# The two arms of a branch in the middle of a fused attention and expert kernel change places

## The chip, the cores and the metric

The kernel runs on one core of a Trainium2 chip. A core has five engines with their own instruction streams: TensorE (PE; its weight loads are shown as PEld), VectorE (DVE), ScalarE (ACT), GpSimd (POOL) and SyncE (SP, which issues most DMAs). A row with a q behind the engine's name is an instruction of that engine's sequencer: a branch, a wait, a DMA issue. The metric is device time in microseconds for one execution.

## The reference

A random-feature attention feeds a layer of eight experts of which each row takes one. There are 4 batches of 576 rows, 8 heads of 64, 2304 rows of 512 in all. Cut to what matters:

```python
proj = np.einsum('bhsd,md->bhsm', x, omega)          # for q and k, scaled
h = proj - sum(x * x) / 2
phi = np.exp(h - h.max(-1)) / np.sqrt(m)
kv = np.einsum('bhsm,bhsd->bhmd', k_p, v)
attn = einsum('bhsm,bhmd->bhsd', q_p, kv) / (einsum('bhsm,bhm->bhs', q_p, k_p.sum(2)) + 1e-06)

logits = x @ w_gate                                   # x: attn as 2304 rows of 512
expert_idx = np.argmax(logits, axis=1)
# the first `capacity` rows of each expert are kept, the others give zero rows
h = np.maximum(x_kept @ w1[e], 0.0)                   # 512 -> 1024
out[i] = gate_w[i] * (h @ w2[e])                      # 1024 -> 512
```

## The kernel before

The attention comes first: keys and values in 18 steps, then queries in 18 steps of 128 rows, with matrix products in float32 on 128 x 128 tiles. Its result goes to a DRAM buffer, and the logits of the experts fall out of the same products.

The expert part works on *items*. An item is a block of 576 rows (SLOTS) that goes through one expert: `mm1` makes the hidden layer in 16 steps, each of 4 x 3 matmuls, since every operand is split into a high and a low part (names ending in hi and lo); `second` makes the five output tiles with `upper` (L898, L899), `lower` (L904) and `rest` (L908), and `finish` scales a tile on ACT (L936) and hands it to `put` (L972), which sends it out by a DMA, four from SP's queue and the fourth tile's from ACT's. Item 0 is the first batch with the expert of row 0. While it runs, the routing is computed, which decides how the other rows are served. Two numbers come out of it, both read from `resd` into registers of every engine: `nd` (L1106), the number of further whole batches in which one expert serves rows, and `nl` (L1107), the number of rows that are left over for such items.

`item` is a generator. The code draws four pieces of item 0 from it (BRANCH_AT is 4), and then branches at L1108 on `nl`. The arm for left-over rows, called the list arm here, writes lists of rows by expert and works through them in up to 11 nested steps, `if ng > 0`, `if ng > 1` and so on, each with its own copy of the code of an item. The other arm draws the rest of item 0 (its last output tile) and then up to three further items, in nested tests `if nd > 0`, `if nd > 1`, `if nd > 2`. Each of these bodies is unrolled. A conditional is built as blocks in every engine's program: a compare-and-branch, the true block right behind it, an unconditional branch at its end, and the false block behind that. A nested test without an else has a small false block too, which brings the semaphores to where the true block would have left them.

With the inputs given `nl` is 0, so the list arm is not taken, and two further items run: `nd` is 2, and the third nested test is false.

The order of instructions is that in which the code is written (a manual schedule). At the end each engine comes to the closing code of L1199: SP waits for all that is outstanding, each engine drains, and POOL collects the others' signals and lets all of them go.

Of the kernel before, what the change touches and what calls it, by code (L numbers as in the profile page):

```python
# [19 lines left out]
B, H, S, D, M = 4, 8, 576, 64, 128  # L20
# [43 lines left out]
def attention_moe(ctx, tc, kT, qT, va, om, wg, w1, w2, cap, ident, tri, desc, lst, tab0, out):  # L64
# [276 lines left out]
    def zero_out(k):  # L341
        if k == 0:
            nc.sync.dma_start(out[SLOTS : SLOTS + REST, :], zero_sb[0:REST, :])
            return
        t = NSUB + 7 * (k - 1)
        z = min(t + 7, NT)
        nc.sync.dma_start(
            out[t * 128 : z * 128, :].rearrange("(a p) d -> p a d", p=128),
            zero_sb.unsqueeze(1).to_broadcast([128, z - t, DM]),
        )  # L350
# [20 lines left out]
    def load_w(i, c, ev, chunks_of="(p k)"):  # L371
        if i == 1:
            src = w1[ds(ev, 1), :, c * 256 : (c + 1) * 256].rearrange(f"o {chunks_of} f -> p (o k) f", p=128)
        else:
            src = w2[ds(ev, 1), c * 256 : (c + 1) * 256, :].rearrange("o (k p) f -> p (o k) f", p=128)
        nc.sync.dma_start(w_raw[i][c], src)

    def split_w_hi(i, c, eng=None):
        split_hi(w_hi[i][c], w_raw[i][c], eng)

    def split_w_lo(i, c, eng=nc.vector, k=None):
        sl = slice(None) if k is None else slice(k, k + 1)
        split_lo(w_lo[i][c][:, sl, :], w_raw[i][c][:, sl, :], w_hi[i][c][:, sl, :], eng)

    def load_idx(start):
        nc.sync.dma_start(big["idx"], tab_d[ds(start, SUB * NSUB), :].rearrange("(i p) c -> p i c", p=SUB))
# [11 lines left out]
    def load_x(rows, b0=0):  # L398
        src = x_d[rows, :].rearrange("(b r) (q c) -> q r b c", r=32, q=4)
        for q in range(4):  # L400
            nc.sync.dma_start(big["xz"][32 * q : 32 * q + 32, b0:, :], src[q])
# [294 lines left out]
    def mm1(f, n, hhi, hlo, hr, nm):  # L696
        xhi, xlo = big["xhi"], big["xlo"]
        whi_, wlo_ = w_hi[1][f // 2], w_lo[1][f // 2]
        fs = slice((f % 2) * 128, (f % 2) * 128 + 128)
        a, z = HALVES[n]  # L700
        sl = slice(a, z)
        pt = bank(turn[0] % 3, f"h{nm}{f}{n}")[:, 0 : z - a]
        turn[0] += 1
        for k in range(4):
            nc.tensor.matmul(pt, whi_[:, k, fs], xhi[:, k, sl], start=(k == 0), stop=False)  # L705
            nc.tensor.matmul(pt, wlo_[:, k, fs], xhi[:, k, sl], start=False, stop=False)  # L706
            nc.tensor.matmul(pt, whi_[:, k, fs], xlo[:, k, sl], start=False, stop=(k == 3))  # L707

        def take():
            w = min(z, 4 * SUB) - a  # L710
            sl = slice(a, a + w)
            parts = [(hhi[:, f, sl], hlo[:, f, sl], pt[:, 0:w])]
            if n == 1:
                parts.append((hr[:, f, 0:REST], hr[:, f, REST:], pt[:, w:]))
            for hi, lo, src in parts:
                nc.scalar.activation(hi, src, AF.Relu)  # L716
            for hi, lo, src in parts:
                nc.vector.scalar_tensor_tensor(lo, src, 0.0, hi.bitcast(F32), op0=ALU.max, op1=ALU.subtract)  # L718

        return take  # L720
# [228 lines left out]
    def listing(n):  # L949
        stop[0] = None  # L950
        for _ in range(n):
            if stop[0] is None:
                stop[0] = next(il, 0)
                if stop[0] == 0:
                    return
# [3 lines left out]
    def item(j):  # L959
        nonlocal row, row_a  # L960
        nm = f"i{j}"
        last = j == B - 1
        hhi, hlo, hr = h0
        if j > 0:
            row_a = nc.scalar.value_load(resd[0:1, 1, j - 1 : j], min_val=0, max_val=N - S)
        out_j = [out[0:SLOTS, :]] * 2 if j == 0 else [out[ds(r, SLOTS), :] for r in (row, row_a)]
        sc = sc_b[:, 0, :] if j == 0 else sc_j[:, j - 1, :]

        def put(i, n, y, out_j=out_j):

            k = int(i == NSUB - 2)
            (nc.sync, nc.scalar)[k].dma_start(out_j[k][i * SUB : i * SUB + n, :], y[0:n, :])  # L972

        def prefetch():
            nonlocal row
            if last:
                return
            ev = nc.sync.value_load(resd[0:1, 0, j : j + 1], min_val=0, max_val=E - 1)
            row = nc.sync.value_load(resd[0:1, 1, j : j + 1], min_val=0, max_val=N - S)
            load_x(ds(row, SLOTS))  # L980
            for c in range(4):
                load_w(1, c, ev)
            evs.append(ev)
            yield

        pre = prefetch()
        for k, (f, half) in enumerate(STEPS[j > 0]):
            mm1(f, half, hhi, hlo, hr, nm)()
            if j == 0:

                listing(5 if k > 4 else 1)
            if 0 < j < B - 1 and k == 0:
                for c in range(4):
                    load_w(2, c, evs[-1])
            if j > 0 and k == 4:
                next(pre, 0)
            if j == 0 and k < 3:
                zero_out(k)
            if half == 0:
                continue  # L1000
            for i, c in HI_AT[j > 0].get(f, ()):
                split_w_hi(i, c)
            for i, c in LO_AT[j > 0].get(f, ()):
                split_w_lo(i, c)
        if j == 0:
            for _ in il:
                pass
            next(pre, 0)
        def ready(c):
            split_w_hi(1, c)  # L1010
            split_w_lo(1, c)

        if 0 < j and not last:
            turn_x(0, NBA)()
            ready(0)
            turn_x(NBA, NB)()
            ready(1)
        if j == B - 2:
            for c in range(4):
                load_w(2, c, evs[-1])  # L1020
        for n, (i, pt) in enumerate(second(hhi, hlo, hr, nm)):
            first_x = turn_x(0, NBA) if j == 0 and n == 1 else None
            finish(i, pt, nm, sc[:, i : i + 1], put)
            if first_x is not None:
                first_x()
            yield

            if j == 0 and n == 2:
                ready(0)
                last_x = turn_x(NBA, NB)  # L1030
                ready(1)
                last_x()
# [69 lines left out]
    first = item(0)  # L1102
    for k in range(BRANCH_AT):
        next(first)
        if k == 1:
            nd = nc.values_load(resd[0:1, 2, 0:1], min_val=0, max_val=B - 1)  # L1106
            nl = nc.values_load(resd[0:1, 2, 1:2], min_val=0, max_val=N)  # L1107
    with ExitStack() as ifs:  # L1108
        cond = ifs.enter_context(tc.If(nl > 0))
        for t in range(BRANCH_AT - 1, NSUB - 1):  # L1110
            nc.sync.dma_start(out[t * SUB : (t + 1) * SUB, :], zero_sb)
        make_lists()
        ng = nc.values_load(res[0:1, 0, 15:16], min_val=0, max_val=NJ)
        for j in range(J):
            nm = f"l{j}"
            ifs.enter_context(tc.If(ng > j))
            ev = nc.sync.value_load(res[0:1, 0, j : j + 1], min_val=0, max_val=E - 1)
            sv = nc.sync.value_load(res[0:1, 1, j : j + 1], min_val=0, max_val=(E - 1) * REG + N)
            load_idx(sv)
            for c in range(4):  # L1120
                load_w(1, c, ev, "(k p)")
            for c in range(4):
                load_w(2, c, ev)
            gather()
            hhi, hlo, hr = h0
            for c in range(4):
                split_w_hi(1, c)
                split_w_lo(1, c)
            for i in range(NSUB):
                for _ in transpose_x(i, nm, SM if i % 2 else None):  # L1130
                    pass
            for f in range(8):
                for half in range(2):
                    mm1(f, half, hhi, hlo, hr, nm)()
                if f % 2:
                    split_w_hi(2, f // 2)
                    split_w_lo(2, f // 2)
            for i, pt in second(hhi, hlo, hr, nm):
                finish(i, pt, nm, idx[:, i, 1:2].bitcast(F32), put_rows)
    with cond.Else():  # L1140
        for _ in first:
            pass
        with ExitStack() as ifs:
            for j in range(1, B):
                ifs.enter_context(tc.If(nd > j - 1))
                for _ in item(j):
                    pass


# [53 lines left out]
```

## Time and profile before

| | us |
|---|---|
| median of 3 runs | 261.96 (260.59 to 262.24) |
| profiled execution | 260.95 |
| its span, first to last instruction | 259.2 |
| PE busy in the span | 253.7 |
| start of the branch at L1108, POOL first, SP last | 130.5 to 151.5 |
| PE's last eight matmuls | 253.38 to 255.36 |

The span is that of the profiled execution; the time that is compared also holds what lies around it, here 1.75 us. Sequencer rows (PEldq, ACTq, ...) are not counted as busy. Where an engine stands still after a branch, no row says so: it is read from the start of its next row.

### The profile page before, as it was taken

What the parts mean: (1) busy time and instruction counts of PE and PEld (TensorE: products, weight loads), DVE (VectorE), ACT (ScalarE), POOL (GpSimd) and SP (SyncE); (2) the same over time, 40 slices, a digit from 0 to 9 for tenths busy, and PEclk for the clock granted to TensorE, in tenths of its full rate; (3) what the DMA queues carried; (4) which work ended last, traced back from release to release, by engine and by line L of the source; (5) the groups of instructions that cost most, each with busy time, mean ns of one, the idle gap of its engine ahead of it and who ended that gap; (6) DMA issues with size and microseconds to landing.
All of it is one profiled execution on the core that took longest, in us unless ns stands there. A gap on an engine that the chain in (4) does not pass through costs nothing. (4 is left out here: it accounts for less than half of the span.)

```text
span 259.2 us, 7581 instructions
## 1 busy us (share of the span) xinstructions
PE 253.7 (98%) x3058; PEld 232.7 (90%) x3058; DVE 167.2 (65%) x351; ACT 148.8 (57%) x374; POOL 42.6 (16%) x61
## 2 busy tenths in 40 slices
PE   7999999999999999999999999999999999999994
PEld 6999999999999999999988789999888999998882
DVE  3999888779999998655763745566850064667500
ACT  3788888899999995326402536552361155524611
POOL 1002000255369896200000000000000000000000
PEclk9999999999999999999999999999999999999999
DMA  7999870034976769990059619992012897950121
GB/s 204 390 382 349 285 254 3 5 122 149 311 234 207 275 169 289 373 390 21 1 134 276 206 49 311 213 286 66 3 40 66 293 245 206 326 164 0 49 93 48
DMA packets 35171, 48.54 MB, mean 187 GB/s; under 512 B 2290, under 2 KB 23410, under 8 KB 35122
## 3 DMA queue, kind: packets, MB, share of 16 engines
q1 hardware_dynamic: 34002, 46.39, 57.0%
q10 hardware_dynamic: 1120, 1.52, 1.9%
q8 instruction: 28, 0.46, 0.7%
q14 instruction: 21, 0.17, 0.2%
HBM read 35.97 MB, written 11.93 MB: 185 GB/s over the span
## 5 line engine op out<-in xcount | busy, mean ns | idle before, releaser
L705 PE MATMUL hi<-xhi,w1hi 128*128 128x256 f32 (+1 forms) x192 | 56.7, 295 | 0.0
L706 PE MATMUL hi<-xhi,w1lo 128*128 128x256 f32 (+1 forms) x192 | 56.4, 294 | 0.0
L707 PE MATMUL hi<-xlo,w1hi 128*128 128x256 f32 (+1 forms) x192 | 56.3, 293 | 0.0
L718 DVE SCALAR_TENSOR_TENSOR hlo<-hi,hhi 128x256 fp32r<-128x256 f32 x48 | 20.2, 420 | 44.4 <-ACT hhi L716 22.4
L716 ACT ACTIVATE hhi<-hi 128x256 fp32r<-128x256 f32 x48 | 18.3, 384 | 36.1 <-PE hi L707 36.1
L898 PE MATMUL yi<-w2hi,hhi 128*128 128x512 f32 x96 | 37.5, 390 | 0.3 <-issue 0.3
L899 PE MATMUL yi<-w2hi,hlo 128*128 128x512 f32 x96 | 37.4, 389 | 0.0
L705 PEld LDWEIGHTS hi<-xhi,w1hi 128*128 128x128 f32 x192 | 36.0, 188 | 0.3
L706 PEld LDWEIGHTS hi<-xhi,w1lo 128*128 128x128 f32 x192 | 36.0, 188 | 0.1
L707 PEld LDWEIGHTS hi<-xlo,w1hi 128*128 128x128 f32 x192 | 36.0, 187 | 0.0
L192 DVE TENSOR_REDUCE mx<-pjk 128x4 f32<-128x512 f32 (+1 forms) x38 | 23.4, 656 | 4.2 <-PE pjk L175 4.0
L837 POOL TENSOR_TENSOR d<-d,mx 128x512 f32<-128x512 f32 x18 | 18.7, 1039 | 42.2 <-DVE mx L192 39.8
L175 PE MATMUL pjk<-om_s,kraw 64*128 64x128 f32 x288 | 23.9, 300 | 0.2
L818 ACT ACTIVATE ex<-pjk,mx 128x128 f32<-128x128 f32 x72 | 20.6, 368 | 6.0 <-DVE mx L192 5.7
L904 PE MATMUL yi<-w2lo,hhi 128*128 128x512 f32 x96 | 23.7, 389 | 0.0
L654 PE MATMUL qacc<-kv_sb,qpT 128*64 128x73 f32 x576 | 22.5, 230 | 0.1
L898 PEld LDWEIGHTS yi<-w2hi,hhi 128*128 128x128 f32 x96 | 18.0, 188 | 4.3 <-issue 0.7
L175 PEld LDWEIGHTS pjk<-om_s,kraw 64*128 64x128 f32 x288 | 20.4, 203 | 1.5 <-DMA kraw<-kT 0.6
L175 PE MATMUL pjq<-om_s,qraw 64*128 64x128 f32 x288 | 21.6, 284 | 0.0
L904 PEld LDWEIGHTS yi<-w2lo,hhi 128*128 128x128 f32 x96 | 18.0, 188 | 3.7
L899 PEld LDWEIGHTS yi<-w2hi,hlo 128*128 128x128 f32 x96 | 18.0, 188 | 3.6
L852 ACT ACTIVATE d<-pjq,mx 128x128 f32<-128x128 f32 x72 | 21.0, 404 | 0.3 <-DVE mx L192 0.3
(148 smaller groups left out, 416.4 us busy)
## 6 DMA issues: line engine op xcount, KB each, us to landing
w1raw<-w SPq DMA_DIRECT2D x16, 512.0 KB, 6.8
w2raw<-w SPq DMA_DIRECT2D x16, 512.0 KB, 5.8
qraw<-qT SPq DMA_DIRECT2D x6, 768.0 KB, 6.3
x_d<-xr SPq DMA_DIRECT2D x18, 256.0 KB, 4.3
v<-va SPq DMA_DIRECT2D x7, 650.0 KB, 6.5
xg<-x_d SPq DMA_DIRECT2D x12, 288.0 KB, 7.6
kraw<-kT SPq DMA_DIRECT2D x5, 576.0 KB, 7.0
out<-ysi SPq DMA_DIRECT2D x9, 256.0 KB, 2.1
```

What stands on the lines that cost most here:

```text
L175: nc.tensor.matmul(banks[i][:, k * M : (k + 1) * M], parts[k][rows, :], om_s[rows, :], start=True, stop=True)
L192: nc.vector.tensor_reduce(mx[:, a : a + src.shape[1]], src, op=ALU.max, axis=AX.X, negate=True)
L654: nc.tensor.matmul(acc[i][r : r + 64, p * ROW : (p + 1) * ROW], qpT[:, r // 64, (4 * i + p) * 64 : (4 * i + p) * 64 + 64], kv_sb[(t * 128 ...
L705: nc.tensor.matmul(pt, whi_[:, k, fs], xhi[:, k, sl], start=(k == 0), stop=False)
L706: nc.tensor.matmul(pt, wlo_[:, k, fs], xhi[:, k, sl], start=False, stop=False)
L707: nc.tensor.matmul(pt, whi_[:, k, fs], xlo[:, k, sl], start=False, stop=(k == 3))
L718: nc.vector.scalar_tensor_tensor(lo, src, 0.0, hi.bitcast(F32), op0=ALU.max, op1=ALU.subtract)
L818: nc.scalar.activation(ex[:, o + k, :], q[0][:, k * M : (k + 1) * M], AF.Exp, bias=mx[:, o + k : o + k + 1], scale=1.0)
L852: nc.scalar.activation(d[:, 4 + k, :], pj[1][:, k * M : (k + 1) * M], AF.Identity, bias=mx[:, 4 + k : 5 + k], scale=1.0)
L898: nc.tensor.matmul(pt, hhi[:, f, sl], w2_at(w_hi, f), start=(f == 0), stop=False)
L899: nc.tensor.matmul(pt, hlo[:, f, sl], w2_at(w_hi, f), start=False, stop=False)
L904: nc.tensor.matmul(pt, hhi[:, f, sl], w2_at(w_lo, f), start=False, stop=(f == 7))
```

## The change

The condition is turned round (`nl > 0` becomes `nl < 1`), and the blocks with it: the rest of the items is now the true block, which stands right behind the compare-and-branch, and the list arm is the else block behind it. The bodies are the same, and so are the semaphores and the number of instructions on each engine. In the new file the outer test is still at L1108, the nested tests over items are at L1111 (before at L1143), those of the list arm at L1116 (before at L1108).

```diff
-    with ExitStack() as ifs:
-        cond = ifs.enter_context(tc.If(nl > 0))
+    with tc.If(nl < 1) as cond:
+        for _ in first:
+            pass
+        with ExitStack() as ifs:
+            for j in range(1, B):
+                ifs.enter_context(tc.If(nd > j - 1))
+                for _ in item(j):
+                    pass
+    with cond.Else(), ExitStack() as ifs:
         for t in range(BRANCH_AT - 1, NSUB - 1):
             nc.sync.dma_start(out[t * SUB : (t + 1) * SUB, :], zero_sb)
         make_lists()
...
-    with cond.Else():
-        for _ in first:
-            pass
-        with ExitStack() as ifs:
-            for j in range(1, B):
-                ifs.enter_context(tc.If(nd > j - 1))
-                for _ in item(j):
-                    pass
```

On PE, around the outer test, the program of before has the list arm right behind the branch (xtrl is a tile of that arm; yi is an output tile of an item, yl one of the list arm), and the rest of item 0 some 3150 rows further on:

```order
L904 MATMUL yi_2800<-w2lo_2317,hhi 128x512 x2
L1108 COMPARE_AND_BRANCH
L1113 TENSOR_LOAD ilres
L1108 COMPARE_AND_BRANCH
L420 MATMUL xtrl_2977<-id_sb,xg 128x128 x4
...
L904 MATMUL yl_8230<-w2lo_2317,hhi 128x512 x2
L1108 UNCONDITIONAL_BRANCH x12
L898 MATMUL yi_8260<-w2hi_2310,hhi 128x512
L899 MATMUL yi_8260<-w2hi_2310,hlo 128x512
```

In the changed program the rest of item 0 follows the branch:

```order
L904 MATMUL yi_2800<-w2lo_2317,hhi 128x512 x2
L1108 COMPARE_AND_BRANCH
L898 MATMUL yi_2829<-w2hi_2310,hhi 128x512
L899 MATMUL yi_2829<-w2hi_2310,hlo 128x512
L898 MATMUL yi_2829<-w2hi_2310,hhi 128x512
```

The list arm has moved from between these rows to behind the items. On ACT, at the end of the last nested item (item 3, the one that is not run here), the program of before ends with the final branches of the items' arm, and the closing code follows them directly:

```order
L936 ACTIVATE ysi_9577<-yi_9552,sc_j 128x512
L936 ACTIVATE ysi_9605<-yi_9580,sc_j 128x256
L972 ISA
L972 DMA out<-ysi_9605 128x512
L1143 UNCONDITIONAL_BRANCH x4
```

In the changed program the list arm follows those branches (its first load, its first nested test, its first casts), some 485 rows of it, and the closing code stands behind them:

```order
L936 ACTIVATE ysi_4146<-yi_4121,sc_j 128x512
L936 ACTIVATE ysi_4174<-yi_4149,sc_j 128x256
L972 ISA
L972 DMA out<-ysi_4174 128x512
L1111 UNCONDITIONAL_BRANCH x4
L1120 TENSOR_LOAD ilres
L1116 COMPARE_AND_BRANCH
L137 CAST w1hi_994<-w1raw_990 128x1024
...
L936 ACTIVATE ysl_9604<-yl_9579,idx 128x512
L1116 UNCONDITIONAL_BRANCH x12
```

What was the end of the program for the items' arm is now its middle; this is so on all five engines.

## Rows read from the trace of the kernel before

**Rows 1.** Page, part 1: busy us (share of the span) xinstructions.
```profile
PE 253.7 (98%) x3058; PEld 232.7 (90%) x3058; DVE 167.2 (65%) x351; ACT 148.8 (57%) x374; POOL 42.6 (16%) x61
```

**Rows 2.** Waits of PE in the whole span: us in total, times, longest us.
```profile
PE yi L898 <- issue: 0.3, 1, 0.3
```

**Rows 3.** Timeline of PE around L1108: start us, us, what [idle before <-releaser].
```profile
145.82 1.98 PE L904 MATMUL yi<-w2lo,hhi 128*128 128x512 f32 x8
...
148.06 0.47 PE L898 MATMUL yi<-w2hi,hhi 128*128 128x512 f32 x1 [0.27 <-issue]
148.37 0.39 PE L899 MATMUL yi<-w2hi,hlo 128*128 128x512 f32 x1
...
149.06 0.40 PE L898 MATMUL yi<-w2hi,hhi 128*128 128x512 f32 x1
```

**Rows 4.** Line L1108: ns minimum/median/maximum, first and last start us.
```profile
L1108 POOLq COMPARE_BRANCH  x1: 45/45/45, 130.5 to 130.5; - x1
...
L1108 PEldq COMPARE_BRANCH  x1: 4317/4317/4317, 143.6 to 143.6; - x1
L1108 ACTq COMPARE_BRANCH  x1: 59/59/59, 149.3 to 149.3; - x1
L1108 DVEq COMPARE_BRANCH  x1: 72/72/72, 150.5 to 150.5; - x1
L1108 SPq COMPARE_BRANCH  x1: 53/53/53, 151.5 to 151.5; - x1
```

**Rows 5.** Line L1143, the nested tests and final branches, whole span.
```profile
L1143 POOLq COMPARE_BRANCH  x4: 34/40/50, 133.6 to 134.2; - x4
...
L1143 DVEq COMPARE_BRANCH  x4: 43/48/74, 153.4 to 244.2; - x4
L1143 SPq COMPARE_BRANCH  x4: 40/43/50, 155.0 to 251.7; - x4
```

**Rows 6.** Line L1143 from 243 us on: the false third test, then the final branch.
```profile
L1143 SPq EVENT_SEMAPHORE  x5: 17/17/17, 251.3 to 251.6; - x5
L1143 DVEq COMPARE_BRANCH  x2: 47/60/74, 243.3 to 244.2; - x2
L1143 SPq COMPARE_BRANCH  x2: 43/46/50, 251.1 to 251.7; - x2
L1143 PEldq COMPARE_BRANCH  x2: 192/2074/3957, 251.1 to 255.7; - x2
L1143 ACTq COMPARE_BRANCH  x2: 38/46/55, 256.5 to 257.1; - x2
L1143 ACTq EVENT_SEMAPHORE  x2: 17/17/17, 257.0 to 257.1; - x2
```

**Rows 7.** Line L1199, the closing code, from 243 us on.
```profile
L1199 POOLq EVENT_SEMAPHORE  x4: 17/17/17, 258.4 to 259.1; - x4
L1199 SPq DRAIN  x3: 7/7/13, 258.3 to 258.6; - x3
...
L1199 PEldq DRAIN  x2: 8/8/8, 255.9 to 258.7; - x2
L1199 ACTq DRAIN  x2: 8/8/8, 257.3 to 258.6; - x2
```

**Rows 8.** Timeline of ACT behind L1108, and its last DMA issue.
```profile
153.95 0.69 ACT L936 ACTIVATE ysi<-yi,sc_b 128x512 f32<-128x512 f32 x1 [2.90 <-PE yi L904]
...
256.16 0.35 ACTq L972 DMA_DIRECT2D out<-ysi  x1
```

**Rows 9.** Waits of SP's queue from 243 us on.
```profile
SPq L1199 <- PEq L1108: 3.1, 1, 3.1
SPq L1199 <- ACTq L1143: 1.5, 1, 1.5
SPq L1199 <- DMA out<-ysi: 0.9, 1, 0.9
```

**Rows 10.** DMA queues from 250 to 260 us: packets, MB, share of 16 engines.
```profile
q8 instruction: 2, 0.03, 1.2%
```

## The prediction

> **What bounds the kernel now.** I read the page's engine part first. TensorE (PE) is busy for 253.7 of 259.2 us, so whatever does not delay PE costs nothing until PE's last matmul is done [rows 1]. Then the waits of PE: once the kernel has started there is one, 0.3 us, on L898, put down to "issue" [rows 2]. Its place in the timeline is the first matmul behind the branch at L1108 [rows 3]. So the branch of this change is the only thing that interrupts PE in the whole middle of the kernel. Third, the branch instructions themselves on each engine [rows 4 to 6], because the change moves code and nothing else. Last, the end: what still runs after PE's last matmul, and which engine the closing barrier waits for [rows 7 to 9].
>
> Why a branch is interesting: its own duration is tens of ns on four engines [rows 4], but the engine's next instruction comes much later. POOL leaves L1108 at 130.5 and shows its next row, an L1143 test, at 133.6: 3.1 us. DVE: 150.5 + 0.07 to 153.4, 2.8 us. SP: 151.5 + 0.05 to 155.0, 3.4 us [rows 4, 5]. On PE the branch's own row holds the time, 4.3 us [rows 4]. None of the three has anything to wait for there; all jump from L1108 over the whole list arm. The tests that fall through, and jumps over a few instructions, show nothing of the kind: the median L1143 branch is 0.04 to 0.05 us on these engines [rows 5]. PE shows one more long one, 3.96 us at 251.1: the third nested test is false (two further items ran, not three) and PE has to jump over some 300 matmuls of the item left out, while ACT and SP have some 50 instructions or fewer to pass and show their next row 0.1 to 0.5 us later [rows 6]. So a jump far ahead costs 3 to 4 us, on every engine for itself, and a near one almost nothing.
>
> **The change, part by part.** All instructions stay; each engine has as many as before.
>
> Taken away in the middle: the far jump at L1108. The condition is now true for this input, and the rest of item 0 stands right behind the branch. For PE this returns what the jump left uncovered. Eight matmuls of this shape that follow each other take 1.98 us, the last one 0.39, so one starts every (1.98 - 0.39) / 7 = 0.227 us. After the row of eight the next start is due at 145.82 + 8 x 0.227 = 147.64 and comes at 148.06: 0.42 us. The four starts after it take 149.06 - 148.06 = 1.00 where 0.91 is due: 0.09. Together **0.5 us** [rows 3]. The other 3.8 us of PE's 4.3 are covered by the matmuls that its sequencer had queued. On ACT, DVE, POOL and SP the removed stall gives nothing: ACT's next work at 153.95 waits for PE's L904 [rows 8], and DVE and POOL have none. SP issues item 1's loads of w2 some 3.4 us sooner, but PE waits for no load anywhere [rows 2], so I count 0; if those loads were late, they could only gain.
>
> Kept: the fall-through tests of the nested items and the false third test (PE 3.96 us, covered by PE's queue up to its last matmul).
>
> Added at the end: before, the Else arm is last, and its final branch goes a few instructions ahead to the closing code of L1199. Now the list arm lies between, so that final branch is as far a jump as L1108 was, on all five engines. What hides it? On POOL and DVE, which reach it at 134.2 and 244.2, everything [rows 5, 6]. On SP, which reaches it at 251.7, a 3.4 us jump ends at 255.1 less 0.5, before the waits that SP has to make anyway for PE and ACT (3.1 and 1.5 us of waiting) [rows 6, 9]. On ACT and PE little. ACT can jump only once it has issued the last output DMA (256.16 + 0.35) and passed the false test, at 257.1 [rows 6, 8]; PE only at 255.7, since its code behind the false test waits for its last matmul [rows 6].
>
> Prices. For PE the 4.3 of L1108. ACT's far jump cannot be read: its next row at L1108 hides it behind PE's matmul, so it is bounded above by 153.95 - 149.4 = 4.6 us. Its nearest rows are POOL, DVE and SP, 3.1, 2.8 and 3.4; I take their mean, 3.1, since ACT's near jumps are like theirs (0.04 us), and keep 2.8 and 4.6 as ends. A gain at the end is excluded, since nothing is removed there.
>
> The sum. Before, SP drains last, at 258.3, after the last output has landed, and POOL opens the barrier at 258.4 [rows 7, 9]; PE and ACT had drained at 255.9 and 257.3 [rows 7]. In the changed kernel everything behind L1108 on PE is 0.5 earlier. SP: 257.8. ACT: 257.1 + 0.04 - 0.5 + 3.1 is 259.7. PE: 255.7 - 0.5 + 4.3 is 259.5. The last is ACT; POOL follows 0.1 later as now, at 259.8, **1.4 us later** than 258.4, and from there to the end of the span nothing changes (0.8 us). Span 260.6; the profiled execution's 260.95 us becomes 262.4. That execution lies at the low end of what was measured: the three runs lie between 260.59 and 262.24, median 261.96, and the four together average 261.4. On that mean the forecast is **262.8 us**. The parts: -0.5 in the middle, +1.9 at the end.
>
> [...]
>
> **The rivals.**
> (a) The end jump is covered or cheap, so that only the 0.5 us in the middle count: 261.4 - 0.5 = 260.9, not slower. Condition: ACT's jump takes under 257.8 - 256.6 = 1.2 us and PE's under 257.8 - 255.2 = 2.6. For it: the present final branch is cheap (ACT's drain follows its branch at 257.1 by 0.2 us [rows 6, 7]), and the closing code might be kept close. Against: no far jump in the trace took under 2.8 us. [...]
> (b) PE becomes the last by far. It lands from the false test's jump at 251.14 + 3.96 = 255.1 and jumps again at 255.7. The trace shows two 16 KB instruction fetches on q8 between 250 and 260 us [rows 10]: one more than that jump's target needs, so PE fetches ahead after landing. If the second jump must wait until that fetch is through, it starts up to 3.96 - 0.6 = 3.4 us later; halfway, 1.7, makes PE's drain 261.2, the end 2.9 us later, time 264.3; the whole of it 4.6, time 266.0. For it: the fetch falls exactly there. Against: the two fetches could overlap. [...] It decides the result once the delay is over 0.2 us.
> (c) ACT's jump costs its upper bound, 4.6: end 2.9 later, 264.3.
> (d) The change does not do what it says: the assembled order of the arms is the same as before, or the condition still jumps. The order of the instructions shows the swap on every engine, so this has almost nothing; it would give 261.4.
>
> **How the numbers follow.** The forecast (far jumps of 2.8 to 3.4 on ACT, 4.0 to 4.3 on PE, end 1.1 to 1.7 later, 262.5 to 263.1) has 0.68; (a) 0.12; (b) 0.13; (c) 0.05; (d) 0.02. A difference under 1% (2.6 us) is about what one cannot tell from no change here, and the runs shown are spread over 1.65 us. The range goes from 261.5, the forecast's low end less half of that spread and a bit, to 264.8, which takes in (c) and the milder half of (b); left out are (a) and the rest of (b). Slower by over 1%: (b) and (c) mostly, 0.15. Faster by over 1%: no case holds it, 0.02 for what I don't see. Within 1%: 0.83.
>
> **What would show it.** No "issue" wait of PE on L898 behind L1108, and on POOL, DVE and SP the next row within 0.2 us of it; the last output's DMA issued 0.5 us earlier, near 255.7; then, after the final branch (now of L1111), 3 us without any row on ACT and a PE branch of 4 us, with the closing drains of ACT and PE behind SP's, near 259.8 and 259.5. Wrong it is if those drains come before SP's (a), if PE's comes after 261 (b), or if PE meets a new wait in the middle.

## The result

The changed kernel takes 262.43 us (median of 18 runs, 261.34 to 264.92), the kernel before 261.56 us beside it (18 runs, 260.11 to 262.24). The ratio is 1.0055 with a 95% interval of 1.0032 to 1.0077; on 261.5 us that is 1.4 us more, between 0.8 and 2.0. The medians alone lie 0.87 us apart and the means 1.35, since the runs of the changed kernel scatter more. So it is slower, by about half a per cent. The profiled execution took 263.32 us, with a span of 261.5.

PE is still the busy engine (page, part 1), with as many instructions as before [rows 1].

```profile
PE 254.0 (97%) x3058; PEld 233.5 (89%) x3058; DVE 167.3 (64%) x351; ACT 148.7 (57%) x374; POOL 42.6 (16%) x61
```

In the middle, the wait on L898 [rows 2] is gone. PE's waits in the whole span are now two, both at the start of the kernel:

```profile
PE wps L304 <- DVE warm L298: 1.2, 1, 1.2
PE pjk L175 <- DMA kraw<-kT: 0.4, 1, 0.4
```

In the timeline of PE around L1108 the matmul behind the branch starts on time: 146.66 + 8 x 0.227 is 148.48, and it starts at 148.47; the next come every 0.22 to 0.23 us. Before, the start came 0.42 us late and the four after it lost 0.09 more [rows 3].

```profile
146.66 1.98 PE L904 MATMUL yi<-w2lo,hhi 128*128 128x512 f32 x8
148.47 0.39 PE L898 MATMUL yi<-w2hi,hhi 128*128 128x512 f32 x1
148.70 0.39 PE L899 MATMUL yi<-w2hi,hlo 128*128 128x512 f32 x1
```

The branch that held PE's sequencer for 4317 ns [rows 4] takes 92 (line L1108; ns minimum/median/maximum, first and last start in us):

```profile
L1108 POOLq COMPARE_BRANCH  x1: 40/40/40, 131.3 to 131.3; - x1
...
L1108 PEldq COMPARE_BRANCH  x1: 92/92/92, 144.4 to 144.4; - x1
...
L1108 DVEq COMPARE_BRANCH  x1: 55/55/55, 151.5 to 151.5; - x1
L1108 SPq COMPARE_BRANCH  x1: 53/53/53, 152.4 to 152.4; - x1
```

And the nested tests follow it at once on POOL, DVE and SP, 0.1 us after L1108, where 2.8 to 3.4 us passed before [rows 4, 5]. Line L1111 from 128 to 155 us:

```profile
L1111 POOLq COMPARE_BRANCH  x4: 34/36/50, 131.4 to 132.0; - x4
...
L1111 DVEq COMPARE_BRANCH  x1: 43/43/43, 151.6 to 151.6; - x1
L1111 SPq COMPARE_BRANCH  x1: 34/34/34, 152.5 to 152.5; - x1
```

At the end, line L1111 from 243 us on, which answers to [rows 6]: PE's final branch, 192 ns before, is now its longest, 4401 ns.

```profile
L1111 SPq COMPARE_BRANCH  x2: 38/44/50, 251.4 to 252.3; - x2
L1111 PEldq COMPARE_BRANCH  x2: 4010/4206/4401, 251.4 to 256.0; - x2
L1111 ACTq COMPARE_BRANCH  x2: 38/44/50, 256.8 to 257.2; - x2
```

The closing code (now L1198) from 243 us on, which answers to [rows 7]:

```profile
L1198 POOLq EVENT_SEMAPHORE  x4: 17/17/17, 260.7 to 261.4; - x4
L1198 SPq DRAIN  x3: 7/7/13, 260.6 to 260.9; - x3
L1198 DVEq DRAIN  x2: 10/34/57, 247.6 to 261.0; - x2
L1198 ACTq DRAIN  x2: 8/44/80, 260.2 to 260.9; - x2
L1198 PEldq DRAIN  x2: 8/40/73, 260.5 to 261.0; - x2
```

ACT drains 3.0 us after its final branch (257.2 to 260.2), where it took 0.2 us before; PE 4.5 us after its own (256.0 to 260.5), where it took 0.2. POOL opens the barrier at 260.7, before at 258.4. But SP is last here too, at 260.6, and that was not foreseen. What SP's queue waits for from 252 us on, which answers to [rows 9], says why:

```profile
SPq L1198 <- DMA out<-ysi: 3.2, 1, 3.2
SPq L1198 <- ACTq L1111: 1.2, 1, 1.2
...
SPq L1198 <- PEq L1108: 0.4, 1, 0.4
```

The wait for the last output's DMA has grown from 0.9 to 3.2 us. That transfer, issued by ACT at L972, took this long to land (from 255 us on; it was 2.1 us before):

```profile
DMA to landing us min/median/max: 4.1/4.1/4.1
```

The two executions cannot be compared by their clock time alone: PE comes to L1108 at 144.4 in this one and at 143.6 in that of before, 0.84 us apart, with the same code ahead of it. Over the twelve profiled executions of this study, in which the code ahead of the branch is the same or nearly so, this moment lies between 142.8 and 144.7 us. Nearly all of the difference arises in the first 14 us: PE's 151st matmul starts at 13.46 us before and at 14.34 here, and from there to L1108 both need 130.1 us. So I count from PE's own rows. PE's last matmul ends at 255.66 (before 255.36): 0.84 us of a later arrival less 0.53 us gained behind L1108. From there to the end of the span it is 5.8 us (before 3.8): 2.0 more. 2.0 - 0.5 is 1.5 us, beside 1.4 measured. TensorE's clock has no part in it: from 14 us to PE's last matmul it is granted in full (1.00) in both executions.

### The profile page after: what moved, and what is told of

Read it like the earlier page. It is cut to its first block, busy times and chain, and to the rows that moved or that the text cites. A ratio compares the mean times of both kernels' runs of the same rounds, so it can differ in the third digit from the quotient of the medians.

```text
span 261.5 us, 7581 instructions
## 1 busy us (share of the span) xinstructions
PE 254.0 (97%) x3058; PEld 233.5 (89%) x3058; DVE 167.3 (64%) x351; ACT 148.7 (57%) x374; POOL 42.6 (16%) x61
## 5 line engine op out<-in xcount | busy, mean ns | idle before, releaser
L898 PE MATMUL yi<-w2hi,hhi 128*128 128x512 f32 x96 | 37.4, 389 | 0.0
L175 PE MATMUL pjk<-om_s,kraw 64*128 64x128 f32 x288 | 24.5, 308 | 0.4 <-DMA kraw<-kT 0.4
L175 PEld LDWEIGHTS pjk<-om_s,kraw 64*128 64x128 f32 x288 | 21.0, 210 | 1.5 <-DMA kraw<-kT 0.7
L898 PEld LDWEIGHTS yi<-w2hi,hhi 128*128 128x128 f32 x96 | 18.0, 188 | 3.6
## 6 DMA issues: line engine op xcount, KB each, us to landing
x_d<-xr SPq DMA_DIRECT2D x18, 256.0 KB, 4.2
out<-ysi SPq DMA_DIRECT2D x9, 256.0 KB, 2.1
```

The source lines that it names most:

```text
L175: nc.tensor.matmul(banks[i][:, k * M : (k + 1) * M], parts[k][rows, :], om_s[rows, :], start=True, stop=True)
L898: nc.tensor.matmul(pt, hhi[:, f, sl], w2_at(w_hi, f), start=(f == 0), stop=False)
```

## The experiments

The theory is the prediction's: a taken branch costs some 3 us on ACT and 4 us on PE if its target is far, wherever it stands; the change takes one from the middle, where PE's queue covers most of it, and puts one at the end, where nothing covers it. A rival: the size or the layout of the program changes the time by itself (the fetch of code, what lies behind what), and the branch is not the cause. A second one: one engine alone makes the end.

All ratios are against the kernel before, with a 95% interval. "Tail" is the time from the end of PE's last matmul to the end of the span: 3.8 us before, 5.8 after. In the seven executions whose final branches are near it lies between 3.8 and 4.1, so a price read from the tail is good to about 0.3 us.

**The branch without the distance.** In both kernels the list arm is cut down to its lists; its up to 11 steps, which do not run with these inputs, are left out. All branches stay, but their targets are near.

```diff
         ng = nc.values_load(res[0:1, 0, 15:16], min_val=0, max_val=NJ)
-        for j in range(J):
+        for j in range(0):
```

On the changed kernel:

> The changed kernel without the list arm's eleven unrolled steps (they do not run with these inputs), so that the final branch passes only some 30 instructions. If the end costs come from the distance jumped: no far jump is left but PE's false third test, PE's last matmul to the end of the span takes 3.8 us as in the kernel before, and the time is 0.5 us under the kernel before, about 260.9. If the order of the arms itself costs (an extra final branch, other waits): about 1 us above the kernel before, as the changed kernel.

Measured: 260.86 us, ratio 0.9997 (0.9973 to 1.002). The tail is 4.0 us and the last output lands in 2.3. PE's final branch is near again (line L1111 from 243 us on):

```profile
L1111 PEldq COMPARE_BRANCH  x2: 193/1935/3677, 250.4 to 255.0; - x2
```

The order of the arms is that of the changed kernel, and what it cost at the end is gone with the distance. On the kernel before:

> The kernel before without the list arm's eleven unrolled steps, so that L1108 is taken but jumps only a few instructions on PE, ACT and SP, some 30 to 40 on DVE and POOL. If distance is what costs: PE's branch at L1108 falls from 4.3 to about 0.1 us, the 0.3 us wait of PE on L898 is gone, time 0.5 us under the kernel before, equal to the changed kernel without the steps. If a taken branch costs whatever its distance: as the kernel before.

Measured: 261.28 us, ratio 0.9997 (0.9971 to 1.0024). Line L1108:

```profile
L1108 PEldq COMPARE_BRANCH  x1: 239/239/239, 143.7 to 143.7; - x1
```

The same taken branch, at the same place and with the same condition, takes 0.24 us and not 4.3, and PE has no "issue" wait left. So the distance makes the price. With it goes a fetch of code: in the kernel before one 16 KB packet of instructions starts on the DMA queue q8 behind PE's branch (143.5 to 148 us; packets, MB, share of 16 engines), and here no instruction packet starts between 133 and 159 us.

```profile
q8 instruction: 1, 0.02, 1.4%
```

The 0.5 us that both should gain over the kernel before is not seen in the medians; 0.998 lies inside both intervals.

A second time on another chip:

> The changed kernel without the list arm's steps once more, since 0.5 us under the kernel before was expected and 0.1 with an interval of 0.7 below to 0.5 above was measured. If the 0.5 us of the middle are real: again below the kernel before, the two runs together by 0.2 to 0.6 us. If something at the end takes them back: no difference.

Measured: 260.99 us, ratio 0.9978 (0.9953 to 1.0003); tail 3.8, PE's final branch 193 ns.

**The far jump told ahead, order of before.** The kernel before, with a hint to PE's sequencer that the branch labelled "lists" will come; it is placed ahead of the last piece of item 0 that is drawn before the branch.

```diff
+HINTED = [mybir.EngineType.PE]
...
     for k in range(BRANCH_AT):
+        if k == BRANCH_AT - 1:
+            with tc.block():
+                tc.mark_branch_hint_location("lists", engines=HINTED)
+                next(first)
+            continue
...
-        cond = ifs.enter_context(tc.If(nl > 0))
+        cond = ifs.enter_context(tc.If(nl > 0, label="lists"))
```

> The kernel before with the list arm in full, and a branch prefetch hint on PE alone, 24 matmuls (some 5 us) ahead of L1108, that names its far target. The code of that output tile stands in a block of its own for it, which adds two near branches. If the far jump's time is the fetch of its target, and can be started ahead: PE's branch at L1108 well under 4.3 us, no PE wait behind it, the end as in the kernel before, time 0.3 to 0.5 us under the kernel before and 1.5 to 2 under the changed one. If the time is something else (the branch being resolved, a restart of the stream) or the hint is dropped: as the kernel before.

Measured: 260.62 us, ratio 0.9976 (0.9953 to 0.9998). The hint is issued at 138.9 us, and the branch (here L1114) takes a third of its time:

```profile
L1114 PEldq COMPARE_BRANCH  x1: 1465/1465/1465, 144.3 to 144.3; - x1
```

The fetch has moved ahead of the branch: from 133 to 144.3 us, where the kernel before has no packet on q8 up to its branch at 143.6, there is one here; it starts at 143.16.

```profile
q8 instruction: 1, 0.02, 0.6%
```

PE's matmuls go on behind the branch without a gap; its only wait in the span is this one, at the start:

```profile
PE wps L305 <- DVE warm L299: 1.2, 1, 1.2
```

The tail is 4.0 us, about as before. By the trace this has the gain of the middle without the price of the end. Again on another chip:

> The kernel before with the prefetch hint once more, to see whether its first result (ratio 0.9976) holds: the middle gives 0.5 us by the trace and the end is that of the kernel before, so 0.2 to 0.8 us under the kernel before. If the first result was scatter: no difference.

Measured: 261.33 us, ratio 0.9985 (0.9961 to 1.0009); the branch takes 1.3 us, no gap, tail 3.8. The interval of this second run takes in no difference, so by the measured times alone the gain is not secured. The hint needs a block of its own around the piece of item 0, so the block was also tried without the hint:

> The kernel with the prefetch hint, without the hint: only the block of its own around the fourth output tile of item 0 stays. If the hint made the gain: PE's branch at the outer test about 4 us and the PE wait behind it, time as the kernel before. If the block made it: as the kernel with the hint, 0.6 us under the kernel before.

Measured: 261.22 us, ratio 0.9994 (0.997 to 1.0018). The branch (here L1113) and PE's wait behind it are back:

```profile
L1113 PEldq COMPARE_BRANCH  x1: 4417/4417/4417, 143.2 to 143.2; - x1
```
```profile
PE yi L899 <- issue: 0.4, 1, 0.4
```

PE loses 0.65 us there, 0.53 of it before the first matmul behind the branch. By PE's rows, then, it is the hint and not the block; the intervals of the two times overlap.

**Both jumps far.** The order of before, with the items inside a further test that is always true, and with an arm behind them that is never taken: 1500 matmuls and 600 small copies on ACT, which only make distance.

```diff
     with cond.Else():
-        for _ in first:
-            pass
...
+        with tc.If(nl < N) as tail:
+            for _ in first:
+                pass
...
+        with tail.Else():
+            fps = bank(SM, "fps")
+            for _ in range(1500):
+                nc.tensor.matmul(fps[:, 0:128], id_sb, id_sb, start=True, stop=True)
+            for _ in range(600):
+                nc.scalar.copy(table, lg[:, 0, 0:1])
```

> The kernel before, with its far jump at L1108, and a filler arm that never runs (1500 matmuls on PE, 600 copies on ACT) between the items and the closing code, so that PE and ACT jump far at the end as well. If the two jumps add: 1.8 to 2 us over the kernel before, about 0.5 over the changed kernel. If the jump in the middle was covered anyway and gave the change nothing: equal to the changed kernel.

Measured: 263.87 us (6 runs), ratio 1.0103 (1.007 to 1.0136): 2.7 us more than before, between 1.8 and 3.6. The far jump in the middle is there, and one at the end as well (the tests over items are at L1144 here):

```profile
L1108 PEldq COMPARE_BRANCH  x1: 3930/3930/3930, 143.7 to 143.7; - x1
```
```profile
L1144 PEldq COMPARE_BRANCH  x2: 3760/4128/4497, 251.0 to 255.5; - x2
```

The tail is 6.2 us, 2.4 more than before, though the arms stand in the old order. That is more than was expected: ACT drains last here, at 260.5, 3.5 us after its final branch. In the middle PE lost 0.30 us at L1108 in this execution, its jump being 0.4 us shorter than in the one of before.

**One engine at a time.** The changed kernel with the short list arm (as in the first experiment), where all jumps are near, and distance for one engine alone at the end of that arm, which is not taken. For ACT:

```diff
-        for j in range(J):
+        for j in range(0):
...
+        for _ in range(600):
+            nc.scalar.copy(table, lg[:, 0, 0:1])
```

> The changed kernel without the list arm's unrolled steps, with 600 copies on ACT alone in the arm that does not run: ACT's final branch is far, PE's is near. If each engine's jump delays the end by itself: ACT's drain comes 3 us after its final branch, the last output lands about 2.1 to 2.4 us after its issue as in the kernel before, and the end lies 5.5 to 5.8 us behind PE's last matmul (3.8 before): 1.3 us over the kernel before. If PE's jump alone makes the cost: as the changed kernel without the steps, no more than 0.5 us over the kernel before.

Measured: 262.34 us, ratio 1.0033 (1.0009 to 1.0057). PE's final branch takes 193 ns. The tail is 5.0 us, 1.0 more than with the short arm. Closing code (here L1200):

```profile
L1200 SPq DRAIN  x3: 7/7/7, 258.6 to 260.0; - x3
...
L1200 PEldq DRAIN  x2: 8/8/8, 256.2 to 260.1; - x2
L1200 ACTq DRAIN  x2: 8/44/81, 259.7 to 260.1; - x2
```

ACT is last, 2.6 us after its branch at 257.1, where 3 were expected; SP had drained at 258.6, since the last output landed in 2.1 us. For PE the same, with 1500 matmuls in the place of the copies:

> The counterpart: 1500 matmuls on PE alone in the arm that does not run, PE's final branch is far, ACT's near. If each jump delays the end by itself: PE's branch 4.3 us, its drain near 5 us behind its last matmul, the end at 5.6 to 5.8, 1.3 us over the kernel before, so that the two engines' costs lie side by side and do not add. If the late landing of the last output in the changed kernel (4.1 us instead of 2.1) comes from PE's fetches, it shows here and not with ACT's jump alone. If ACT's jump alone makes the cost: no more than 0.5 us over the kernel before.

Measured: 261.71 us, ratio 1.0032 (1.0005 to 1.0058). The tail is 5.3 us, 1.3 more than with the short arm. The final branch (L1111) and the closing code (here L1201), from 243 us on:

```profile
L1111 PEldq COMPARE_BRANCH  x2: 3770/3846/3921, 250.3 to 254.8; - x2
```
```profile
L1201 SPq DRAIN  x3: 7/7/7, 258.9 to 259.2; - x3
...
L1201 ACTq DRAIN  x2: 8/8/8, 256.2 to 259.2; - x2
L1201 PEldq DRAIN  x2: 8/8/8, 258.9 to 259.3; - x2
```

ACT is through at 256.2. PE and SP end together at 258.9, SP because the last output took this long (L972, from 252 us on):

```profile
DMA to landing us min/median/max: 3.5/3.5/3.5
```

So one engine's jump alone costs 1.0 (ACT) or 1.3 us (PE) at the end, and the changed kernel, where both are far, 1.8 (5.8 against 4.0): they run side by side. Neither engine alone makes the end.

**The changed kernel again,** beside the two one-engine kernels on one chip:

> The changed kernel as it is, on the same chip as the three others, for comparison: 0.8 to 2.0 us over the kernel before; no PE wait behind L1108, the end 5.5 to 6 us behind PE's last matmul, with a PE branch of 4.4 us, ACT's drain 3 us behind its final branch and a landing of the last output of about 4 us.

Measured: 262.25 us, ratio 1.004 (1.0011 to 1.0068), which is 1.0 us more than before, between 0.3 and 1.8. Tail 5.8, PE's final branch 4441 ns, ACT 3.05 us from its branch to its drain, the last output 4.1 us. The end of the first profile was not an accident of one execution.

## Why the prediction was right

**The middle, 0.5 us back on PE.** Right in the traces: 0.53 us. The rest of the 4.3 us was covered, as stated. PE's rows repeat it: from the start of its outer branch to the end of its last matmul it needs 111.25 us in all nine executions in which that branch is near or hinted, 111.78 in that of before, 111.89 in the one with the block alone and 111.54 with both jumps far. The losses of 0.53, 0.65 and 0.30 us are what is left of jumps of 4.3, 4.4 and 3.9 us when 3.6 to 3.8 us are covered. By the measured times the effect is at the edge of what can be measured: the five runs of kernels without an uncovered jump in the middle or a far one at the end measured 0.9997, 0.9997, 0.9978, 0.9976 and 0.9985, on average 0.9987, or 0.35 us. That the stalls of DVE, POOL and SP there were worth nothing is right too: they are gone, and nothing but PE's 0.5 us came of it.

**The final branch becomes a far jump on all engines.** Right. Covered on POOL, DVE and SP, as forecast. DVE drains at 247.6, 3 us after its branch, and nobody waits for that.

**ACT's price of 3.1 us,** taken from the other engines' jumps, since no row showed ACT's: measured 3.0 here and 3.05 the second time, 2.6 with ACT's jump alone, 3.5 with both jumps far in the old order. The upper bound of 4.6 (rival (c)) did not come.

**PE's price of 4.3 us,** from the same branch at L1108: measured 4.4, 4.5 with both jumps far in the old order, and 3.9 when PE jumps alone.

**The end 1.9 us later, counted from PE's last matmul:** 2.0. The sum was right, but the step **"the last is ACT"** was not quite. PE's jump was the longer by more than forecast, and one term was missing: the last output, which SP waits for, landed after 4.1 us, not after 2.1. SP drained at 260.6, PE at 260.5, ACT at 260.2. The three ends lie within half a microsecond, so the sum missed little. That is luck: SP's end was put some 2 us too early, and it cost the sum only 0.15 us because PE and ACT were almost as late. The forecast's SP end, 0.5 us sooner than before, held only in kernels where PE's jump is near.

Why that transfer is late can be read from the DMA queues' packets. Windows of 256.3 to 258 us and, in the second fence, 259 to 260.2 us of the changed kernel (packets that start there, MB, share of 16 engines):

```profile
q10 hardware_dynamic: 112, 0.22, 37.6%
q8 instruction: 1, 0.02, 7.8%
```
```profile
q10 hardware_dynamic: 9, 0.02, 5.6%
```

q10 carries the output. One packet of instructions on q8 stands among its packets; its time is 7.8% of 16 engines x 1.7 us, 2.1 us. It runs from 256.95 to 259.07, and the last nine packets of the output, a sixteenth of its 144, start from 259.05 on, one after the other. Of the other 135 all but seven had ended by 258.2, and those seven by 259.01. The packets' own records show the same in each of the four executions with PE's final jump far (landing 4.1, 4.1, 4.1 and 3.5 us): the last train of output packets starts within 0.02 us of the end of that fetch. In the other eight the last packet on q8 ends before the output's first one starts, and the landing takes 2.0 to 2.3 us. That the train stood behind the fetch on one and the same DMA engine is likely from this, but not shown: the records do not name the engine.

**Rival (a),** the end jump is cheap: refuted by the rows of L1111 and the drains. The row of a near or untaken branch lasts 34 to 92 ns in most views above and 190 to 240 for PE's near jumps, that of PE's far one 4401. A packet of instructions follows the final branch of four engines by about 1 us in the changed kernel: on q8 at 256.95 us behind PE's (256.0), on q14 at 245.56, 253.25 and 258.27 behind those of DVE (244.6), SP (252.3) and ACT (257.2). Between 143 and 160 us, where PE, ACT, DVE and SP jump far in the kernel before, nine packets of instructions start there (three on q8, six on q14), and none in the changed kernel.

**Rival (b),** PE's second jump waits for the fetch that runs after the first: refuted. The price was 4.4 us where 4.3 was forecast. The q8 packet that follows PE's landing from the false third test runs from 256.11 to 257.38, and the one of the final jump starts at 256.95, before that is through. In the kernel with PE's jump alone the first ends at 255.56 and the second starts at 255.76, 0.96 us after the branch, as in the changed kernel (256.0 to 256.95): the overlap does not delay the second fetch. It may still lengthen it. PE's jump takes 3.9 us when PE jumps alone, where nothing overlaps its fetch, and 4.4 to 4.5 in the other three executions, where the earlier fetch on q8 overlaps it and ACT jumps too; the difference lies in the fetch itself, 1.6 against 2.1 to 2.2 us. Which of the two lengthens it was not separated. ACT's jump takes 2.6 us alone and 3.0 to 3.5 beside PE's.

**Rival (d),** no change as built: refuted by L1108, 92 ns.

**Layout or size by itself:** refuted. Old order with distance behind the items is slow (1.0103), new order without distance is not (0.9997, 0.9978).

Open stays why PE's jump at L1108 took 4.3 and 4.4 us in two executions and 3.9 in a third; the loss follows from its length.

## What to carry to other kernels

A taken branch with a far target and no hint ahead of it cost 2.6 to 4.5 us here, on every engine that took it, and one with a near target at most 0.5. Far is some 300 matmuls or more on PE and some 480 instructions or more on ACT, near some 50 instructions or fewer; where it changes between them no run shows. Putting the arm first only moved that jump to the arm's end (on PE from 4.3 us at L1108 to 4.4 at L1111). So look at what covers it at both places: in the middle PE's queued matmuls hid 3.8 of 4.3 us, at the end nothing hid PE's 4.4 us or ACT's 3.0. Where the order is free, leave the far jump where the bounding engine has work queued, keep the arms that are seldom taken short, or announce the jump: the old order with the hint to PE was the fastest of the kernels that keep the whole list arm (0.9976 and 0.9985).

## What was not expected of the hardware

- A hint ahead of the branch cut PE's far jump from 4.3 us to 1.5 and 1.3.
- With PE's far jump beside it a 256 KB output landed after 3.5 to 4.1 us instead of 2.0 to 2.3, and the fetch that lay across the output took 1.6 to 2.2 us, against 0.9 to 1.4 for those on q8 at the end of the kernels in which PE's final jump is near.
- The time at which PE comes to the same branch, after the same code, differs by up to 1.9 us from one profiled execution to another, more than the whole effect of the change. Between the executions of the two kernels it is 0.84 us, and nearly all of that arises in the first 14 us (the same matmul starts at 13.46 us before and at 14.34 after).
